# Attention and a softplus feed-forward on one core: new constants for the planner that orders the work of five engines

## The chip, the cores and the metric

One core of a Trainium2 chip runs the whole kernel. The metric is device time in microseconds (us), from one execution to the next of the same program; lower is better. TensorE (PE) does the matmuls, VectorE (DVE), ScalarE (ACT) and GpSimd (POOL) the element work, SyncE (SP) and GpSimd's queue start most transfers.

## What is computed

```python
def reference(q, k, v, moe_w_in, moe_w_out):          # float32
    # q, k, v: 8 batches, 8 heads, 576 positions, 64 wide, in 9 chunks of 64
    scores = q_c @ k_c.T / sqrt(64)                   # inside each chunk
    attn = softmax(scores)
    x = (attn @ v_c), heads side by side              # 4608 tokens x 512
    h = x @ w_in                                      # 512 x 2048
    g = maximum(h, 0) + log1p(exp(-abs(h)))           # softplus
    return g @ w_out                                  # 4608 x 512
```

## The kernel before

**Tiles and stages.** The 4608 tokens are 36 tiles of 128 (a tile is two chunks, all heads), in nine rows of four tiles (m = 0 to 8). The 2048 hidden columns are 16 pieces (fc). A block is one m with one fc, named m * 16 + fc. Each float32 product is made of three matmuls of rounded parts (hi times hi, hi times lo, lo times hi), so each operand needs a high part (a copy) and a low part (a subtraction). The first three rows run plainly, piece by piece: `gemm1` (line 640: x times w_in), softplus (line 648), its high and low part `g_hi` (line 652) and `g_lo` (line 656), then `gemm2` (line 830: g times w_out) one block later. The first two blocks are halved: half-blocks a0 and a1 use tiles 0 and 1, blocks 0 and 1 then use tiles 2 and 3. The other six rows run two at a time, in three supers, with products of sums (line 776) built from sums over x (lines 754, 761 and 766) and over w_in.

**Attention.** Tiles 0 to 3 go through TensorE one by one (transposes, scores, maximum, exp, sum, `att_norm`, transpose, product with v, high and low part of x at lines 617 and 621). The others go in pairs of tiles through bursts: `burst` multiplies the weights of one pair of tiles with v (line 604) and computes the scores of the next pair (line 516). Bursts stand at blocks 4, 8, 15 and then at `BURST_AT`, later at places inside the supers. q and k of these tiles are turned by VectorE (lines 493 and 503), the weights by VectorE too (line 540), in some tiles partly by transfers (line 551, those not in `SWAP_DVE`).

**Weight decode.** The 32 weight pieces are units, in the order in0, in1, out0, in2, out1, in3, out2 and so on: unit 3 is in2, unit 4 is out1. A unit is loaded by SP into one of three raw tiles, shifted by two bytes (`w_load`, lines 269 and 274). Then its top half (`w_top`, line 282, on ScalarE if in `TOP_ACT`, else GpSimd) and its low half (`w_low`, line 292, ScalarE) are taken out, added on VectorE (`w_add`, line 297), copied to the high part (`w_hi`, line 324, on GpSimd if in `HI_POOL`) and subtracted to the low part (`w_lo`, line 328, on GpSimd if in `LO_POOL`). All 32 are decoded while the first sixteen blocks run.

**The order.** Every step is a task of `Plan` with an engine, a cost, the tasks it needs, buffers that it takes, and an urgency `urg`. A list scheduler plays the tasks through in modelled time, and each engine's instructions are emitted in the order in which it picked them; the engines then run that order, waiting for one another by semaphores:

```python
can = [t for t in wait[eng] if ready[t["name"]] <= now + 1e-9 and has_room(t, now)]
...
t = min(can, key=lambda t: (t["urg"], t["seq"]))
...
if t["port"]:
    end = port = max(now, port) + cost
```

The last two lines are the planner's account of an exclusion between VectorE and GpSimd: every GpSimd task has `port`, and of VectorE's tasks only `w_add` has it. Plain block g is due at `30 + 5.2 * g`; a unit's urgency is its block's due time less 4 plus `DECODE_AT[u]` (for out pieces the block is later by `WO_AFTER`), a load's is that less `LEAD` or, for the first ones, taken from `LOAD_AT` (q and k of tiles 0 to 3, v of tiles 0 to 3, then units 0 to 5). Tile i of the first four has urgency `ATT_AT[i]` and up. For a burst due at d, q and k have `d - QK_URG`, v `d - V_URG`, or `d + V_LATE` if it has a place of its own (`HOMES`), swaps `d - SW_URG`; the sums over x have `d - X_URG`. In the plain rows the sums over w_in (lines 695 to 715) and the stores of w_in's parts (line 726) to a scratch tensor have `d + W_URG`. `ON_POOL` names the q, k and v that GpSimd's queue loads instead of SP. `NORM_POOL` and `GLO_POOL` name the tiles and blocks whose normalisation and whose g_lo GpSimd does, `TK` the tiles whose turned k VectorE copies instead of ScalarE. After 120 us of modelled time an engine may stay idle up to `HOLD` for an urgent task. TensorE's order of blocks and bursts is fixed in a list; it takes its PSUM from two `pa` tiles (scores, gemm1, x) and four `po` tiles (gemm2).

## Time and profile before

| | |
|---|---|
| time, median of 3 runs | 836.19 us (836.0 to 836.98) |
| profiled execution: its own time, its span | 835.88 us, 833.9 us |
| TensorE, VectorE, ScalarE, GpSimd busy | 819.0, 522.3, 382.0, 327.6 us |
| granted TensorE clock | 1.00 |
| first matmul of gemm1 | 24.46 us |
| burst at block 4, 8, 15, 22 starts | 52.47, 78.20, 122.64, 163.03 us |
| first product of the three supers | 316.30, 487.58, 660.80 us |

The span goes from the first to the last instruction of the profiled execution; the time also holds what lies around it. Busy time of TensorE counts its pipelined matmuls with modelled ends, so a busy TensorE says only that matmuls follow one another.

### The profile page before, as it was taken

To read this page: it belongs to the slowest core of one execution; us is meant where nothing else is said; L and a number is where in the kernel's file an instruction comes from. 1 tells how busy PE (TensorE), PEld (TensorE's weight loads), DVE (VectorE), ACT (ScalarE), POOL (GpSimd) and SP (SyncE) were. 2 spreads that over 40 slices of the span, in tenths; PEclk is the share of its full clock that TensorE was granted. 3 is DMA by queue.
4 is the path that set the end of the run, shared out by engine and by line. 5 is a ranking of instruction groups with operands and counts; after the bars stand their busy time and mean duration, and the time that the engine had idled before them with its cause. 6 is when DMAs were issued, how large, how long until landed. Compare 5 with 4: busy or idle time off the path is not lost.

```text
span 833.9 us, 15342 instructions
## 1 busy us (share of the span) xinstructions
PE 819.0 (98%) x5745; PEld 671.3 (80%) x5745; DVE 522.3 (63%) x871; ACT 382.0 (46%) x612; POOL 327.6 (39%) x380
## 2 busy tenths in 40 slices
PE   9899999999999999999999999999999999999998
PEld 7677778888888878888887878888888888888886
DVE  3998987178568677475577877583867732232322
ACT  4867764345443564353444544433544443333322
POOL 1654569776998652311324521232230021311100
PEclk9999999999999999999999999999999999999999
DMA  9997657755475455777558427758452155354332
GB/s 215 259 211 171 185 164 206 221 115 168 87 192 124 111 150 189 190 217 201 161 187 217 112 91 234 192 168 241 140 200 92 51 208 183 115 181 159 101 101 75
DMA packets 189513, 137.34 MB, mean 165 GB/s; under 512 B 152704, under 2 KB 166272, under 8 KB 186496
## 3 DMA queue, kind: packets, MB, share of 16 engines
q1 hardware_dynamic: 178400, 86.68, 39.0%
q0 software_dynamic: 10896, 49.56, 19.0%
q8 instruction: 45, 0.74, 0.4%
q14 instruction: 28, 0.23, 0.1%
q10 hardware_dynamic: 144, 0.13, 0.0%
HBM read 100.14 MB, written 35.13 MB: 162 GB/s over the span
## 4 chain that ended last, share of the span: by engine, by line
PE 84%; DVE 5%; DMA 4%; SPq 3%; issue 1%; ACT 1%; POOL 1%; DVEq 0%; POOLq 0%
PE po L830 42%; PE pa L776 27%; PE pa L640 11%; PE pa L604 2%; DMA q<-in_q_dram 2%; SPq L355 2%; PE pa L516 2%; DMA raw<-in_moe_w_out_dram 1%; DMA raw<-in_moe_w_in_dram 1%; DVE qe L503 1%; DVE ends L297 1%; DVE wib L297 1%; SPq L551 0%; POOL g_lo L656 0%; SPq L269 0%
## 5 line engine op out<-in xcount | busy, mean ns | idle before, releaser
L795 POOL TENSOR_TENSOR wib<-wib 128x512 f32<-128x512 f32 x48 | 63.5, 1323 | 279.1 <-ACT wib L782 273.8
L830 PE MATMUL po<-late,g_hi 128*128 128x512 f32 x538 | 165.8, 391 | 0.0
L656 DVE TENSOR_TENSOR g_lo<-ends,g_hi 128x512 fp32r<-128x512 f32 x96 | 66.3, 691 | 92.1 <-ACT g_hi L652 88.2
L830 PEld LDWEIGHTS po<-late,g_hi 128*128 128x128 f32 x538 | 100.3, 188 | 21.3 <-DVE late L328 0.3
L776 PE MATMUL pa<-wi_hi,xb 128*128 128x512 f32 x368 | 113.4, 389 | 0.0
L652 ACT CAST g_hi<-ends 128x512 fp32r<-128x512 f32 x96 | 59.3, 618 | 114.0 <-PE po L830 108.5
L830 PE MATMUL po<-wo_hi,g_hi 128*128 128x512 f32 x288 | 109.7, 393 | 0.6 <-POOL wo_hi L324 0.6
L830 PE MATMUL po<-wo_lo,g_hi 128*128 128x512 f32 x288 | 108.7, 390 | 0.6 <-POOL wo_lo L328 0.6
L830 PE MATMUL po<-late,g_lo 128*128 128x512 f32 x287 | 108.1, 390 | 1.0 <-issue 0.7
L830 PE MATMUL po<-wo_hi,g_lo 128*128 128x512 f32 x288 | 108.5, 389 | 0.0
L776 PE MATMUL pa<-wib,xb 128*128 128x512 f32 x432 | 104.2, 394 | 0.7 <-DVE wib L766 0.7
L540 DVE STREAM_TRANSPOSE eT<-qe 32x256 f32<-32x256 f32 x224 | 97.4, 435 | 5.1 <-POOL qe L591 1.9
L776 PEld LDWEIGHTS pa<-wib,xb 128*128 128x128 f32 x432 | 79.2, 188 | 21.8 <-ACT wib L782 5.5
L795 DVE TENSOR_TENSOR wib<-wib,pa 128x512 f32<-128x512 f32 x72 | 49.4, 686 | 62.0 <-PE pa L776 47.3
L776 PEld LDWEIGHTS pa<-wi_hi,xb 128*128 128x128 f32 x368 | 68.9, 188 | 14.5 <-issue 0.2
L776 PE MATMUL pa<-wi_lo,xb 128*128 128x512 f32 x184 | 71.6, 389 | 0.0
L648 ACT ACTIVATE u<-pa 128x512 f32<-128x512 f32 (+1 forms) x50 | 29.0, 580 | 87.3 <-PE pa L640 80.1
L782 ACT COPY wib<-pa 128x512 f32<-128x512 f32 x72 | 39.8, 588 | 62.4 <-PE pa L776 62.4
L803 ACT ACTIVATE ends<-pa 128x512 f32<-128x512 f32 x48 | 28.7, 598 | 80.9 <-PE pa L776 55.7
L830 PEld LDWEIGHTS po<-late,g_lo 128*128 128x128 f32 x287 | 53.9, 188 | 13.1 <-issue 1.1
L830 PEld LDWEIGHTS po<-wo_lo,g_hi 128*128 128x128 f32 x288 | 54.0, 188 | 12.1 <-POOL wo_lo L328 1.1
L830 PEld LDWEIGHTS po<-wo_hi,g_hi 128*128 128x128 f32 x288 | 53.7, 188 | 12.0 <-POOL wo_hi L324 0.8
(184 smaller groups left out, 1362.5 us busy)
## 6 DMA issues: line engine op xcount, KB each, us to landing
xb<-scratch POOLq DMA_DIRECT2D x23, 1024.0 KB, 5.6
xb<-scratch POOLq DMA_DIRECT2D x24, 768.0 KB, 7.3
spill<-ends SPq DMA_DIRECT2D x21, 512.0 KB, 5.7
ends<-spill SPq DMA_DIRECT2D x21, 512.0 KB, 3.3
out_dram<-raw SPq DMA_DIRECT2D x35, 256.0 KB, 2.8
raw<-in_moe_w_in_dram SPq DMA_DIRECT2D x16, 512.0 KB, 5.3
raw<-in_moe_w_out_dram SPq DMA_DIRECT2D x16, 512.0 KB, 4.6
scratch<-ends SPq DMA_DIRECT2D x16, 512.0 KB, 3.4
```

Of the source, the lines that this page charges most:

```text
L297: nc.vector.tensor_tensor(low, low, live.pop(("top", u)), op=ALU.add)
L355: eng.dma_start(dst[p0 : p0 + rows], src[b, :, s0 : s0 + rows, :].rearrange("h s d -> s h d"))
L540: nc.vector.transpose(live["eT", i][d : d + BL, tb], e[s : s + BL, kb])
L640: nc.tensor.matmul(ph, wt[:, c, :], x[:, ts_, c, :], start=(n == 0), stop=(n == 3 * KC - 1))
L648: nc.scalar.activation(w["u"], w["ph"], AF.Softplus)
L652: nc.scalar.copy(w["hi"], w["u"])
L656: (nc.gpsimd if pool else nc.vector).tensor_tensor(w["lo"], w["u"], w["hi"].bitcast(F32), op=ALU.subtract)
L776: nc.tensor.matmul(w["bank"][BANK[k]], wts[:, q, c, :], x[:, c, :], start=k < NX and c + n == 0, stop=c == 1 and n == 2, skip_group_check= ...
L782: nc.scalar.copy(tmp_of(n), w["bank"][n])
L795: (nc.gpsimd if what in MIX_POOL else nc.vector).tensor_tensor(out, a, b, op=op)
L803: nc.scalar.activation(u_tiles(j)[i], src, AF.Softplus)
L830: nc.tensor.matmul(pos[w["m"]][t], terms[n][0][:, j * P : (j + 1) * P], terms[n][1], start=(w["first"] and n == 0), stop=n == 2 and (w["la ...
```

## The change

Constants only. Sets that choose an engine: `TK`, `HI_POOL`, `LO_POOL`, `TOP_ACT`, `NORM_POOL`, `GLO_POOL`, `SWAP_DVE`, `ON_POOL`. Urgencies and places: `DECODE_AT`, `ATT_AT`, `LOAD_AT`, `WO_AFTER`, `QK_URG`, `V_URG`, `V_LATE`, `W_URG`, `X_URG`, `SW_URG`, `LEAD`, `HOLD`, and the third of `BURST_AT`, from block 31 to 32. No function is edited; every engine's order comes out of the planner anew.

```diff
--- before.py
+++ after.py
@@ -41,7 +41,7 @@
     FLYING = 8
     AHEAD = 3.2
     WARM_UNTIL = 90.0
-    HOLD = 0.55
+    HOLD = 0.5
     HOLD_FROM = 120.0
 
     def __init__(self, **pools):
@@ -869,17 +869,17 @@
     NOFF = 3
     T0 = 30.0
     TG = 5.2
-    DECODE_AT = (-10.4, -5, -1, -3, -5, 1, -3, 3, -40.8, -60, 2.4, -5)
-    TK = ()
+    DECODE_AT = (-20, -2.3, -8.9, -2, -60, 1.4, 0.2, -3, 2.1, -5, 5.9, 0)
+    TK = (1, 2)
     KS = 0.2
-    ATT_AT = (-34.3, -4.4, -52.4, -194.6)
-    LOAD_AT = (-89.2, -65.7, -51.7, -58.6, -27.7, -49.7, -47.4, -42.4, -48.8, -0.1, -8.7, 2.1, 5.1, 35.8)
-    HI_POOL = (0, 1, 2, 3, 4, 5, 6, 7, 11, 13, 16, 18, 19, 20, 21, 24, 25, 30, 31)
+    ATT_AT = (-52.5, 101.4, -70.6, -226.8)
+    LOAD_AT = (-104.1, -66.1, -54.8, -64.2, -28.7, -42.9, -41.8, -37.3, -47.5, -9.7, -24.4, -1.0, -1.7, 22.2)
+    HI_POOL = (0, 1, 2, 3, 5, 6, 7, 8, 11, 12, 13, 15, 17, 18, 19, 20, 21, 25, 31)
     WHOLE = (4, 5, 9)
-    SWAP_DVE = (4, 7, 8, 10, 11, 12, 13, 14, 15, 16, 17, 19, 20, 21, 22, 23, 24, 25, 26, 27, 28, 29, 30, 31, 32, 33, 34, 35)
+    SWAP_DVE = (4, 7, 9, 10, 11, 13, 14, 15, 16, 17, 19, 20, 21, 22, 23, 24, 25, 26, 27, 28, 29, 30, 31, 32, 33, 34, 35)
     SWAP_ACT = ()
     BEGIN = (4, 8, 15)
-    BURST_AT = (22, 26, 31, 36, 40, 44)
+    BURST_AT = (22, 26, 32, 36, 40, 44)
     HOMES = {(n, i): ("early", 2 * (i - FIRST_BLK) + j) for i in (5, 7) for j, n in enumerate("qk")}
     HOMES.update({("v", 4): ("early", 4), ("v", 5): ("early", 5)})
     HOMES.update({("v", 8): ("xb", 0), ("v", 9): ("xb", 1), ("q", 11): ("xb", 4), ("k", 11): ("xb", 5)})
@@ -899,12 +899,12 @@
         ("v", 10, 0, (0, 1)), ("v", 11, 0, (0, 1)), ("q", 13, 0, (2, 3)), ("k", 13, 0, (2, 3)),
         ("v", 16, 1, (0, 1)), ("v", 17, 1, (0, 1)), ("v", 18, 1, (2, 3)), ("v", 19, 1, (2, 3)))})
     LOAD_POOL = ()
-    TOP_ACT = (1, 4, 5, 6, 7, 8, 9, 11, 12, 13, 15, 17, 18, 19, 21, 22, 24, 25, 26, 28, 29, 30, 31)
+    TOP_ACT = (1, 4, 5, 6, 7, 8, 9, 12, 13, 14, 15, 17, 18, 19, 20, 22, 24, 25, 26, 28, 30)
     LOAD_AFTER = "q0"
-    LO_POOL = (2, 3, 4, 8, 9, 11, 13, 17, 19, 21, 23, 25, 26, 28)
-    NORM_POOL = (0, 3, 4, 5, 6, 8, 10, 15, 18)
-    GLO_POOL = (0, 1, 2, 7, 8, 10, 13, 14, 15, 17, 18, 19, 21, 22, 23, 26, 30, 34, 35, 36, 38, 42, 44, 45, 47)
-    WO_AFTER = 1.3
+    LO_POOL = (2, 3, 4, 7, 9, 11, 12, 13, 14, 17, 18, 19, 22, 23, 26, 29, 31)
+    NORM_POOL = (0, 3, 4, 5, 6, 8, 10, 13, 14)
+    GLO_POOL = (0, 3, 6, 7, 8, 10, 13, 17, 19, 20, 21, 22, 23, 25, 26, 34, 39, 44)
+    WO_AFTER = 1.1
     IN_SUPER = ([0, 2], [0, 5], [0, 7], [1, 4])
     XS_POOL = ()
     XL_POOL = ()
@@ -913,18 +913,18 @@
     QK_AFTER = "v3"
     V_AFTER = "load10"
     K6_AFTER = "load13"
-    QK_URG = -16.8
+    QK_URG = -54.3
     T_URG = -0.6
-    V_URG = 26.0
-    V_LATE = 27.1
-    W_URG = 7.6
+    V_URG = 111.0
+    V_LATE = 31.9
+    W_URG = 0.2
     QUEUE = dict(wd="SP", wo="SP", ring="POOL", us="SP", ul="SP")
     ISSUE = dict(ACT=0.4, SP=0.57, POOL=0.6)
-    ON_POOL = (['k', 11], ['k', 14], ['k', 15], ['k', 17], ['k', 30], ['q', 16], ['q', 21], ['q', 29], ['q', 30], ['v', 8], ['v', 10], ['v', 11], ['v', 16], ['v', 20], ['v', 21], ['v', 26], ['v', 27], ['v', 29], ['v', 33], ['v', 34], ['v', 35])
+    ON_POOL = (['k', 9], ['k', 11], ['k', 15], ['k', 17], ['k', 29], ['q', 10], ['q', 14], ['q', 16], ['q', 21], ['q', 30], ['v', 8], ['v', 11], ['v', 12], ['v', 13], ['v', 16], ['v', 24], ['v', 26], ['v', 27])
     LOADER = {(n, i): "POOL" for n, i in ON_POOL}
-    X_URG = 97.0
-    SW_URG = -34.0
-    LEAD = 5
+    X_URG = 130.5
+    SW_URG = -57.4
+    LEAD = 9.39571158947384
 
     blocks = [
         dict(m=m, fc=fc, first=fc == 0, last=fc == FC - 1, g=m * FC + fc, name=m * FC + fc, tiles=range(TPM))
```

## Rows read from the trace of the kernel before

**Rows 1.** Windows: stretch, length, busy us (count) of PE, PEld, DVE, ACT, POOL; then TensorE clock.
```profile
0.00:24.00 24.00, 21.61 (x286) 17.90 (x286) 10.82 (x23) 12.16 (x21) 5.77 (x12) 1.00 1.09 229
24.00:122.00 98.00, 91.02 (x646) 73.31 (x647) 91.19 (x153) 69.65 (x114) 52.37 (x49) 1.00 0.76 196
122.00:300.00 178.00, 178.00 (x1612) 147.40 (x1611) 115.09 (x207) 82.82 (x129) 142.71 (x166) 1.00 0.59 157
300.00:833.90 533.90, 528.41 (x3205) 432.63 (x3203) 305.24 (x491) 217.39 (x350) 126.79 (x153) 1.00 0.53 159
```

**Rows 2.** TensorE in order of time: start, us, instruction, [idle before <-releaser].
```profile
29.86 0.71 PE L640 MATMUL pa<-xb,wi_hi 128*128 128x256 f32 x4 [1.45 <-DVE xb L621]
...
34.93 0.73 PE L830 MATMUL po<-wo_hi,g_hi 128*128 128x512 f32 x2 [0.58 <-POOL wo_hi L324]
36.29 0.74 PE L830 MATMUL po<-wo_lo,g_hi 128*128 128x512 f32 x2 [0.63 <-POOL wo_lo L328]
...
40.14 1.07 PE L640 MATMUL pa<-xb,wi_hi 128*128 128x512 f32 x4
...
76.17 2.09 PE L640 MATMUL pa<-xb,wib 128*128 128x512 f32 x8 [0.69 <-DVE wib L328]
...
114.80 1.45 PE L640 MATMUL pa<-xb,wib 128*128 128x512 f32 x5 [1.06 <-DVE wib L328]
```

**Rows 3.** VectorE in order of time, decode instructions of the ramp.
```profile
28.42 0.70 DVE L328 TENSOR_TENSOR wi_lo<-wib,wi_hi 128x512 fp32r<-128x512 f32 x1
...
57.93 0.68 DVE L297 CUSTOM_DVE_ANT_0 wib<-wib,ends 128x1024 uint16<-128x1024 uint16 x1
...
59.85 0.68 DVE L328 TENSOR_TENSOR wo_lo<-wib,wo_hi 128x512 fp32r<-128x512 f32 x1
...
74.70 1.42 DVE L328 TENSOR_TENSOR wib<-ends,wib 128x512 fp32r<-128x512 f32 x1
...
112.90 1.24 DVE L297 CUSTOM_DVE_ANT_0 ends<-ends 128x1024 uint16<-128x1024 uint16 x1
```

**Rows 4.** The window 24 to 122 us, decode adds (line 297) alone.
```profile
24.00:122.00 98.00, 24.27 (x31) 1.00 0.76 196
```

**Rows 5.** The same window, decode subtracts (line 328) alone; VectorE, then GpSimd.
```profile
24.00:122.00 98.00, 15.60 (x15) 19.36 (x14) 1.00 0.76 196
```

**Rows 6.** The same window, softplus low parts (line 656); VectorE, then GpSimd.
```profile
24.00:122.00 98.00, 7.93 (x9) 10.14 (x8) 1.00 0.76 196
```

**Rows 7.** GpSimd in order of time, four of its instructions.
```profile
31.41 1.30 POOL L328 TENSOR_TENSOR wi_lo<-wib,wi_hi 128x512 fp32r<-128x512 f32 x1
...
58.67 0.78 POOL L282 CAST ends<-raw 128x512 f16<-128x512 bf16 x1 [3.02 <-DVE wib L297]
...
304.88 3.51 POOL L656 TENSOR_TENSOR g_lo<-u,g_hi 128x512 fp32r<-128x512 f32 x1 [6.67 <-ACT g_hi L652]
...
315.18 1.28 POOL L656 TENSOR_TENSOR g_lo<-u,g_hi 128x512 fp32r<-128x512 f32 x1 [0.56 <-ACT g_hi L652]
```

**Rows 8.** TensorE in order of time, beside the third row of rows 7.
```profile
308.44 0.50 PE L830 MATMUL po<-late,g_lo 128*128 128x512 f32 x1 [0.38 <-POOL g_lo L656]
```

**Rows 9.** SP in order of time: DMA issues of the start.
```profile
16.84 0.98 SPq L269 DMA_DIRECT2D raw<-in_moe_w_in_dram  x2
...
23.22 1.19 SPq L274 DMA_DIRECT2D raw<-in_moe_w_out_dram  x1
```

**Rows 10.** SP in order of time, ahead of the burst at block 22.
```profile
124.48 4.94 SPq L486 DMA_DIRECT2D q<-in_q_dram  x8
...
153.95 4.77 SPq L486 DMA_DIRECT2D xb<-in_q_dram  x8
158.77 3.21 SPq L726 DMA_DIRECT2D scratch<-wib  x4
```

**Rows 11.** VectorE in order of time, tile 11 before that burst.
```profile
161.18 0.71 DVE L493 STREAM_TRANSPOSE qe<-xb 128x512 f32<-128x512 f32 x1 [6.83 <-DMA scratch<-wib]
```

**Rows 12.** TensorE in order of time, scores of tile 11 in that burst.
```profile
164.79 0.68 PE L516 MATMUL pa<-ka,qe 64*64 64x64 f32 x31
```

## Prediction

> **What bounds the kernel now.** I read the windows first, to see where TensorE is idle [rows 1]: 24.00 - 21.61 = 2.4 us in the first 24 us, 98.00 - 91.02 = 7.0 us from 24 to 122, nothing from 122 to 300, and 533.90 - 528.41 = 5.5 us after that, much of it the last store behind the last matmul. The granted clock is 1.00 throughout. Both kernels do the same work, so the most that an order can win is about 7 us in the stretch from 24 to 122, in which the weights are decoded while the first block row already runs (the ramp, below), and a little behind it.
>
> TensorE's timeline then says what ends its waits there [rows 2]. The first block's second half-block, at 29.86, waits for VectorE's xb: that is the release of a `pa` bank. The second product of the ramp waits twice for GpSimd's decode of out1, 0.58 us before 34.93 and 0.63 before 36.29. At 76.17 and 114.80 the matmuls wait 0.69 and 1.06 us for VectorE's low part of a w_in piece. VectorE is the engine behind the ramp: it is busy 91.19 of 98 us, ScalarE 69.65, GpSimd 52.37 [rows 1].
>
> Part of what keeps VectorE busy is not its own work. Instructions of one form take two durations: a decode subtract (L328) 0.68 us at 59.85 and 1.42 at 74.70, a decode add (L297) 0.68 us at 57.93 and 1.24 at 112.90 [rows 3]. Over the ramp, against 0.68 us each: 24.27 - 31 x 0.68 = 3.2 us for the adds, 15.60 - 15 x 0.68 = 5.4 us for the subtracts, and 7.93 - 8 x 0.68 = 2.5 us for g_lo, two of whose nine are half-size [rows 4 to 6]. About 11 us of VectorE's 91 are stretch. It comes from GpSimd, and it works both ways: the g_lo that GpSimd began at 304.88, beside VectorE's sums over x, took 3.51 us, the one at 315.18 took 1.28 [rows 7]. The Trainium skill (SBUF — State Buffer, Who interferes with whom) states the rule: a VectorE instruction with two SBUF inputs and a GpSimd instruction that reads SBUF exclude each other, and the later one waits for the whole of the other. The trace agrees: 3.51 against 1.28 us.
>
> **The change part by part.** All of it is constants: sets that choose an engine, and urgencies that choose an order.
>
> *Engines in the ramp.* LO_POOL gains units 7, 12, 14, 18, 22, 29, 31 and loses 8, 21, 25, 28. Unit 31 is decoded after 122 us, so two low parts net leave VectorE: -2 x 0.68 = -1.4 us there, +2 x 1.28 = +2.6 us on GpSimd. GLO_POOL up to block 16 loses 1 (a half block), 2, 14, 15 and gains 3, 6, one and a half blocks net: +1.0 us on VectorE, -1.9 us on GpSimd. TOP_ACT drops 11, 21, 29, 31 and takes 14, 20: two tops net, 2 x 0.78 = +1.6 us on GpSimd [rows 3, 7]. HI_POOL swaps four for four. VectorE's own work changes by -0.4 us, GpSimd's by +2.3 us. GpSimd's 52 us stretched VectorE by 11, or 0.21 us for each; 2.3 x 0.21 = +0.5 us. Together +0.1 us: the moves by themselves are worth nothing.
>
> *TK.* Two copies of kT go from ScalarE to VectorE before 16 us. VectorE is busy 10.82 of the first 24 us [rows 1]; its idle time hides them. Without that cover they would cost about 0.7 us each.
>
> *Loads of units 3 and 4.* The new urgencies put unit 4 (out1) ahead of unit 3 (in2), and give unit 4's decode -60. A load needs one of three raw tiles: in2 was the second of the pair issued at 16.84, out1 came at 23.22 [rows 9]. Exchanged, out1 is some 6 us earlier and both its waits go: -0.58 - 0.63 = -1.2 us. in2 is 6 us later: its low part was done at 31.41 + 1.30 = 32.7 on GpSimd [rows 7], so 38.7, and its first matmul stood at 40.14 [rows 2], or 38.9 with TensorE 1.2 us earlier. in2 is late next, by nothing yet. Bounds -1.2 to 0; I take -1.2, as the two rows are 0.2 us apart on the good side.
>
> *Tile 1 of the attention last.* Its urgency goes from -4.4 to 101.4, behind tiles 0, 2 and 3 and the first decodes, and the first block needs tiles 0 and 1. What can be put ahead of it on VectorE is the work of two tiles, some five instructions of 0.7 us: at most +3 us. The other way, tiles 2 and 3 finish earlier and the 1.45 us before 29.86 go; but that matmul also needs unit 1, whose low part ended at 28.42 + 0.70 = 29.12 [rows 3], so at most -0.7. I take 0: unit 1 sets this point either way.
>
> *The order around the stretch.* Two VectorE instructions directly ahead of TensorE's waits were stretched: the subtract at 74.70 by 0.74 us, ahead of a wait of 0.69; the add at 112.90 by 0.56, ahead of one of 1.06 [rows 2, 3]. An order that keeps GpSimd from beside them wins the smaller of each pair, 0.69 + 0.56 = 1.25 us. Bounds: 0 (others are stretched instead) and -5.8 (all the ramp's 7.0 us but the 1.2 above). I take -1.25, the only waits whose rows show a stretch right before them.
>
> *g_lo of blocks 42, 45, 47 to VectorE.* Block 45's is the one of 3.51 us, and TensorE waited 0.38 us for it [rows 7, 8]. On VectorE its urgency (-1) puts it ahead of the sums over x, at 0.69 us: -0.4 us. The other g_lo moved to VectorE behind the ramp are hidden: it is busy 115 of 178 us from 122 to 300 [rows 1].
>
> *Transfers.* QK_URG, V_LATE, SW_URG, W_URG, ON_POOL and the swaps of tiles 8, 9 and 12 reorder SP's queue from 115 us on. TensorE is never idle from 122 to 300, so nothing can be won there; what can be lost is the third rival. LEAD brings loads from unit 6 on forward by 4.4 us of urgency, but free raw tiles hold them back: nothing. X_URG, V_URG and HOLD: what they move was first in its queue already, or is not in front of TensorE: nothing; the bound is the 5.5 us of idle time behind 300 us, tail included.
>
> Sum: 0.1 - 1.2 + 0 - 1.25 - 0.4 = -2.75 us. The profiled execution took 835.88 us (833.9 of span, 2.0 around it), so 833.1; it lies 0.3 us below the median of 836.19. Forecast: **833.4 us**. No change is taken as within 0.2%, 1.7 us: 834.5 to 837.9.
>
> **The rivals.**
>
> *The ramp's gain is swallowed.* VectorE is behind the ramp's last wait too, the one before 114.80. If it gets through its 91 us no sooner, what is won at 35 us is lost again there, and only the 0.4 us at 308 remain: 835.8. For it speaks that the moves come to +0.1 us; against it that 11 of the 91 us are stretch, which an order can change.
>
> *VectorE and GpSimd together fill the ramp (slower).* GpSimd's 52 us and VectorE's 55 adds, subtracts and g_lo at 0.68 us, 37 us, exclude each other: 89 of 98 us. Each low part moved adds 1.28 - 0.68 = 0.6 us to that, each top 0.78, each g_lo moved back takes off 0.6: 1.2 + 1.6 - 0.9 = +1.9 us. From the point at which that sum, and not VectorE alone, is what the ramp goes by, the time is 836.2 + 1.9 = 838.1. A rule of the Trainium skill (Perfetto Trace Analysis, Optimizing Scalar/DVE Operations) warns of it: offloading from VectorE to GpSimd might not help, since they share a read port.
>
> *A burst waits for its q (slower).* q of tile 11 was issued at 153.95, ahead of four weight stores at 158.77 that took 3.21 us of SP; its transpose ended at 161.18 + 0.71 = 161.9, and the burst used it at 164.79 [rows 10 to 12]. By the new urgencies (due 144.4 + 54.3 = 198.7, against 161.4 for these stores and 176.3 for v of tile 10) the stores and four transfers of v go first, 3.2 + 2.5 us, while q of tile 10 (4.9 us) leaves SP for GpSimd: 0.8 us later, in time by 2.1, with TensorE some 2.4 us earlier. If q10's move frees nothing, the burst stands 5.7 - 2.9 = 2.8 us, and the gains being there or not, 836.2 or 839.
>
> *The first block starts late (slower).* If tile 1 is done later than unit 1 (29.12), each us goes straight to the end: with +3 us and no gain but the 0.4, 838.8.
>
> **How the numbers follow.** The forecast's case 0.44, its own range 830.5 to 834.5. Swallowed 0.25 (834.6 to 837). Both engines 0.11 (837 to 839, half of it past 837.9). A burst 0.12 (836 to 840, two thirds past). The first block 0.08 (836 to 839, most of it past). Faster 0.44, slower 0.06 + 0.08 + 0.06 = 0.20, same 0.36. For 8 in 10 the range reaches into all of them: 830.0 to 838.8.
>
> **What would show it.** Right: no wait for wo_hi and wo_lo near 35 us; TensorE idle 4.5 us or less from 24 to 122; adds and subtracts nearer 0.68 us in the mean; block 45's g_lo on VectorE. Wrong: the first block later than 27 us with nothing won behind it; idle time before a burst's L604 or L516 between 160 and 300 us; VectorE as full and as stretched as before, up to 120 us.

## The result, and the profile after

The changed kernel takes 838.02 us (median of 15 executions, 836.18 to 841.15) against 836.19 for the kernel before on the same chip (15 executions, 835.18 to 837.81): a ratio of 1.0025, 95% interval 1.0013 to 1.0037. It is slower by 1.8 us, where 833.4 was forecast. The time lies inside the range, the direction is wrong.

The profiled execution took 840.45 us, its span is 838.7; it is one of the longer ones. The windows, to be set against [rows 1]:

```profile
0.00:24.00 24.00, 21.59 (x278) 17.72 (x278) 11.36 (x21) 9.71 (x17) 4.57 (x11) 1.00 1.11 233
24.00:122.00 98.00, 90.86 (x661) 75.16 (x653) 89.40 (x154) 67.71 (x112) 56.41 (x54) 0.98 0.72 193
122.00:300.00 178.00, 176.07 (x1572) 145.35 (x1574) 111.22 (x200) 80.66 (x127) 142.69 (x174) 1.00 0.58 154
300.00:839.00 539.00, 533.15 (x3264) 436.20 (x3255) 303.24 (x497) 221.47 (x354) 105.62 (x126) 1.00 0.53 159
```

VectorE is relieved a little in the ramp (91.19 to 89.40 us) and GpSimd is busier by 4.0, yet TensorE is no busier. Two things are new: the granted clock is 0.98 there, and from 122 to 300 us, where TensorE had no idle time, it now has 1.93 us. A busy share doesn't place the loss, so the next reading sets the start of the same matmul in both traces against each other:

| place (start before, us) | after - before, us |
|---|---|
| first half-block, G1_a0 (24.46) | +2.07 |
| second half-block, G1_a1 (29.86) | +5.43 |
| first gemm2 (31.37) | +6.47 |
| block 2 (40.14) | +4.71 |
| block 14 (112.67) | +1.33 |
| block 15 (119.50) | +2.20 |
| 168.25 | +2.22 |
| 256.70 | +4.15 |
| 310.86 | +3.46 |
| end of the third super (805.49) | +4.72 |

So the ramp behind its start does gain, 4.71 - 1.33 = 3.4 us; all of that and more was lost ahead of it, and 1.93 us are lost once more near 250 us. What is left of the 4.72 is small: +0.87 at block 15, -0.69 near 308 us and +1.26 in the supers, where the largest wait, 0.88 us before 413.22, has no releaser in the trace. TensorE's timeline shows both main losses, and answers [rows 2]:

```profile
26.53 0.72 PE L640 MATMUL pa<-xb,wi_hi 128*128 128x256 f32 x4
...
33.86 1.78 PE L375 MATMUL pa<-ident 128*128 128x128 f32 x8 [1.96 <-DVE xb L621]
35.29 1.20 PE L640 MATMUL pa<-xb,wi_hi 128*128 128x256 f32 x4
...
37.84 0.62 PE L830 MATMUL po<-wo_hi,g_hi 128*128 128x512 f32 x2
...
117.03 2.12 PE L640 MATMUL pa<-xb,wib 128*128 128x512 f32 x8 [1.84 <-DVE wib L328]
...
255.32 0.47 PE L640 MATMUL pa<-xb,wi_hi 128*128 128x512 f32 x1 [1.77 <-DVE qe L566]
```

The two waits for wo_hi and wo_lo near 35 us are gone, as forecast, and so is the one of 0.69 us before 76.17. Two waits of the kernel before that the prediction did not list, at the bursts of blocks 4 and 8, are gone with it:

```profile
57.55 1.16 PE L640 MATMUL pa<-xb,wi_hi 128*128 128x512 f32 x4 [0.55 <-DVE qe L566]
...
80.83 0.69 PE L516 MATMUL pa<-ka,qe 64*64 64x64 f32 x32 [0.66 <-DVE ka L493]
```

These three places are most of the 3.4 us (0.71, 0.86 and 0.87 us of it). The wait before 114.80, of 1.06 us, has grown to 1.84 in this execution (117.03). And the wait for VectorE's xb, 1.45 us before 29.86, is now 1.96 before 33.86. It is the same bank of `pa`: it holds tile 3's x until VectorE's xl3 (line 621) has read it. ScalarE and VectorE in order of time say why that is late:

```profile
27.29 0.78 ACT L282 CAST ends<-raw 128x512 f16<-128x512 bf16 x1
27.94 0.66 ACT L292 ACTIVATE wib<-raw 128x512 int32<-128x512 uint32 x1
28.61 1.28 ACT L648 ACT_TABLE_LOAD   x1
29.91 0.38 ACT L648 ACTIVATE u<-pa 128x256 f32<-128x256 f32 x1
30.19 0.58 ACT L617 CAST xb<-pa 128x512 fp32r<-128x512 f32 x1
```

```profile
29.53 1.14 DVE L297 CUSTOM_DVE_ANT_0 wib<-wib,ends 128x1024 uint16<-128x1024 uint16 x1
30.59 0.68 DVE L328 TENSOR_TENSOR wi_lo<-wib,wi_hi 128x512 fp32r<-128x512 f32 x1
31.29 1.79 DVE L503 STREAM_TRANSPOSE qe<-q 32x256 f32<-32x256 f32 x4
33.11 1.29 DVE L621 TENSOR_TENSOR xb<-pa,xb 128x512 fp32r<-128x512 f32 x2
```

Unit 4, decoded early now, puts its top and low half (27.29 and 27.94) ahead of the softplus and its table load on ScalarE, so tile 3's xh3 runs at 30.19. VectorE meanwhile takes unit 4's add, unit 1's low part (28.42 before, [rows 3]) and the q transpose Tq4, 1.79 us long, and xl3 follows at 33.11. TensorE has nothing to do, and the eight filler matmuls (line 375) that the planner put ahead of G1_a1 write the same bank, so they wait for it too and then take 35.29 - 33.86 = 1.43 us more. That makes up the 3.36 us by which G1_a1 is later than G1_a0: 0.39 is G1_a0 itself, whose last matmuls wait until 27.82 for tile 1's low part, 1.54 lies between tile 3's product with v (28.53, before 26.07) and the end of the wait (33.86, before 29.86), 1.43 is the filler. The granted clock in steps of 2 us from 32:

```profile
32.00:34.00 2.00, 0.14 (x1) 0.14 (x2) 1.94 (x5) 2.00 (x5) 0.68 (x1) 1.00 0.22 82
34.00:36.00 2.00, 2.00 (x11) 2.00 (x12) 1.99 (x5) 0.61 (x2) 0.60 (x1) 0.55 0.61 173
36.00:38.00 2.00, 2.00 (x12) 2.00 (x11) 0.99 (x3) 0.00 (x0) 1.28 (x2) 0.59 0.89 313
```

TensorE was busy 0.14 of 2 us, and the clock then fell to about half, the 1.2 GHz level. G1_a1 took 37.84 - 35.29 = 2.55 us; before, 31.37 - 29.86 = 1.51. The filler was slowed too, as the experiment with q21 will show. The sum to block 2: 2.07 + 3.36 (G1_a1 behind G1_a0) + 1.04 (clock, in G1_a1 alone) - 1.76 (out1's waits) = 4.71.

The loss at 255 us begins on VectorE with one g_lo; GpSimd's rows stand beside it:

```profile
249.95 3.90 DVE L656 TENSOR_TENSOR g_lo<-u,g_hi 128x512 fp32r<-128x512 f32 x1 [3.53 <-ACT g_hi L652]
```

```profile
246.12 4.61 POOL L486 DMA_DIRECT2D xa<-in_q_dram  x8 [3.82 <-DVE qe L493]
250.75 2.55 POOL L695 TENSOR_TENSOR raw<-wib 128x512 f32<-128x512 f32 x2
253.37 3.13 POOL L707 TENSOR_TENSOR ends<-raw 128x256 f32<-128x256 f32 x4
```

The g_lo, 0.69 us when nothing disturbs it, starts 0.80 us ahead of two two-input instructions of GpSimd that follow its issues of q21, and ends 0.55 us behind the second, though GpSimd's next additions, at 253.37, begin before that. The burst's maxima queue behind it on VectorE, and TensorE waits 1.77 us. The transfer itself is in time; issuing it from GpSimd at that place, as the kernel before did at another moment, is what did harm.

### The profile page after: what moved, and what is told of

It is laid out like the page before. It is cut to its first block, busy times and chain, and to the rows that moved or that the text cites. A ratio compares the mean times of both kernels' runs of the same rounds, so it can differ in the third digit from the quotient of the medians.

```text
span 838.7 us, 15358 instructions
## 1 busy us (share of the span) xinstructions
PE 821.7 (98%) x5751; PEld 674.4 (80%) x5751; DVE 515.2 (61%) x870; ACT 379.5 (45%) x608; POOL 309.3 (37%) x363
## 4 chain that ended last, share of the span: by engine, by line
PE 86%; DVE 7%; ACT 2%; DMA 2%; issue 1%; POOL 0%; SPq 0%; DVEq 0%; POOLq 0%; ACTq 0%
PE po L830 42%; PE pa L776 26%; PE pa L640 13%; PE pa L604 2%; PE pa L516 1%; DVE ends L297 1%; DMA xb<-scratch 1%; DVE qe L503 1%; PE po L375 1%; DVE g_lo L656 1%; DMA spill<-ends 1%; PE po L416 1%; DVE eT L540 0%; ACT u L648 0%; DVE wib L795 0%
## 5 line engine op out<-in xcount | busy, mean ns | idle before, releaser
L540 DVE STREAM_TRANSPOSE eT<-qe 32x256 f32<-32x256 f32 x216 | 93.9, 435 | 3.0
L830 PEld LDWEIGHTS po<-wo_hi,g_lo 128*128 128x128 f32 x288 | 54.1, 188 | 11.4
```

Source lines behind the costliest of these rows:

```text
L540: nc.vector.transpose(live["eT", i][d : d + BL, tb], e[s : s + BL, kb])
L830: nc.tensor.matmul(pos[w["m"]][t], terms[n][0][:, j * P : (j + 1) * P], terms[n][1], start=(w["first"] and n == 0), stop=n == 2 and (w["la ...
```

## The experiments

Each kernel was timed against the kernel before on the same chip:

| kernel | us, median (range, executions) | before | ratio, 95% interval |
|---|---|---|---|
| changed kernel | 838.02 (836.18 to 841.15, 15) | 836.19 | 1.0025, 1.0013 to 1.0037 |
| tile 2 behind | 835.51 (834.48 to 837.20, 11) | 835.81 | 0.9999, 0.9991 to 1.0008 |
| no filler | 836.19 (832.71 to 839.73, 12) | 835.81 | 1.0011, 0.9998 to 1.0024 |
| q21 on SP | 836.25 (833.31 to 839.74, 12) | 835.81 | 1.0006, 0.9990 to 1.0021 |
| q14 and q21 on SP | 835.61 (833.11 to 838.78, 12) | 835.94 | 0.9995, 0.9983 to 1.0006 |
| old engines | 838.81 (837.95 to 844.13, 6) | 835.49 | 1.0054, 1.0032 to 1.0075 |
| tile 2 behind, q14, q21 on SP | 835.69 (834.03 to 838.22, 12) | 835.49 | 1.0001, 0.9991 to 1.0011 |
| tile 2 behind, tile 3 first | 835.81 (833.70 to 838.46, 12) | 836.41 | 0.9997, 0.9985 to 1.0009 |
| all three | 832.77 (832.32 to 834.54, 6) | 835.49 | 0.9970, 0.9958 to 0.9982 |

A constant set back alone makes the planner order everything anew, so that nothing is held still. The edits below change the emitted order in a few places and leave the rest; taking q14 and q21 off GpSimd left the planner's modelled end as it was. That modelled end, no measurement, is itself 0.4 us later with the new constants than with the old.

Starts against the kernel before, in each kernel's own profile, in us:

| place | changed | again | tile 2 behind | no filler | old engines | q14, q21 on SP | all three |
|---|---|---|---|---|---|---|---|
| G1_a0 | +2.07 | +2.33 | +1.57 | +0.42 | +0.96 | +0.96 | +1.16 |
| G1_a1 | +5.43 | +5.44 | +2.93 | +2.00 | +3.36 | +4.60 | +0.71 |
| block 2 | +4.71 | +4.96 | +3.10 | +1.77 | +1.62 | +3.72 | +0.90 |
| block 14 | +1.33 | +1.54 | +0.66 | -1.67 | +0.32 | +0.25 | -1.37 |
| 168.25 | +2.22 | +0.74 | -0.64 | -3.10 | +0.60 | -0.89 | -1.71 |
| 203.15 | +2.22 | +2.82 | -0.64 | -1.14 | +0.60 | -0.88 | -1.71 |
| 256.70 | +4.15 | +4.79 | -0.73 | +0.81 | +2.55 | -0.97 | -1.79 |
| 805.49 | +4.72 | +5.40 | -1.12 | +1.74 | +2.87 | -0.30 | -1.69 |

**The changed kernel again**, unedited: a second profile, 841.14 us.

> The changed kernel once more, unedited, for a second profile. If the late start is a property of the order, half-block a1 starts again some 5 us later than in the kernel before (35.3 against 29.9 us), and the stall of 1.9 us in front of the block after the burst at 40 is there again. If these are accidents of one execution (the runs of the changed kernel spread over 5 us, those of the kernel before over 2.6), a1 is within 2 us of 29.9 or the stall is missing.

The start is the same (+5.44 at G1_a1), and so is the loss at 250 us. The wait before block 15 is absent; a new one of 1.78 us stands at 203, behind another g_lo held by GpSimd's chain, VectorE's row first, then GpSimd's:

```profile
198.60 4.91 DVE L656 TENSOR_TENSOR g_lo<-u,g_hi 128x512 fp32r<-128x512 f32 x1 [2.11 <-issue]
```

```profile
195.98 3.45 POOL L486 DMA_DIRECT2D q<-in_q_dram  x6
199.44 1.30 POOL L695 TENSOR_TENSOR raw<-wi_hi,wi_lo 128x512 f32<-128x512 f32 x1
200.69 1.05 POOL L591 TENSOR_TENSOR qe<-qe,den 128x512 f32<-128x512 f32 x1
201.69 1.26 POOL L695 TENSOR_TENSOR raw<-wi_hi,wi_lo 128x512 f32<-128x512 f32 x1
```

Here the issues are those of q14. What is common to both executions is the start and the kind of stall; which stalls fall due differs.

**Tile 2 behind.** Tile 2's product and x parts are emitted behind G1_a1, which has no need of them:

```diff
+moved = [p for p in out if p[1]["name"] in ("V2", "xh2", "xl2")]
+out = [p for p in out if p[1]["name"] not in ("V2", "xh2", "xl2")]
+n = [p[1]["name"] for p in out].index("G1_a1") + 1
+out[n:n] = moved
```

> The changed kernel with the v product of attention tile 2 and its two x parts emitted right behind half-block a1 instead of ahead of it, so that a1 no longer waits for the release of that PSUM tile. Theory A (the late start passes through to the end): a1 starts near 31.3 us, when unit 1 is decoded, 4 us earlier than 35.3; the first blocks and the time follow by 2 us or more (836 or less). Theory B (VectorE's decode sets TensorE's place at 122 us): a1 is as early, but the block at 119.5 + 2.2 us stands within 0.7 us of there, and the time changes by less than 0.8 us.

G1_a1's shift is now 1.36 us larger than G1_a0's, not 3.36; TensorE is kept going by filler from 30 us, and the clock stays up. The window of the profile:

```profile
30.00:32.00 2.00, 2.00 (x19) 2.00 (x20) 1.94 (x4) 1.69 (x4) 1.47 (x2) 1.00 1.19 309
```

G1_a1 comes at 32.79 and not near 31.3, as expected: unit 1's low part is done at 30.84 and the bank is free, but 26 filler matmuls, emitted for the longer planned gap, run from 29.86 on. They keep the clock up and delay the matmul that they stand ahead of. Not all of the gain is kept either: block 0's other half, which needs tile 2, now waits in its turn (+4.66 where G1_a1 has +2.93), so that at block 2 the shift is 1.5 us larger than at G1_a0, against 2.6. The time falls to that of the kernel before, 2.5 us below the changed kernel's, as theory A has it; theory B's block at 119.5 would stand near +2.2 and is at -0.74. In its profile the g_lo of the 250 us stall, which VectorE starts 0.81 us ahead of GpSimd's chain this time, escapes; VectorE, then GpSimd:

```profile
247.09 0.69 DVE L660 TENSOR_TENSOR g_lo<-u,g_hi 128x512 fp32r<-128x512 f32 x1 [3.52 <-ACT g_hi L656]
```

```profile
243.27 4.61 POOL L490 DMA_DIRECT2D xa<-in_q_dram  x8 [3.82 <-DVE qe L497]
247.90 2.55 POOL L699 TENSOR_TENSOR raw<-wib 128x512 f32<-128x512 f32 x2
```

**No filler** ahead of G1_a1 (other filler stays):

```diff
-self.gap = start - last if start < self.WARM_UNTIL else 0.0
+self.gap = start - last if start < self.WARM_UNTIL and t["name"] != "G1_a1" else 0.0
```

> The changed kernel without the eight filler matmuls in front of half-block a1. They wait for the same PSUM tile as a1 does, so they run behind the wait and not in it. If they matter only by their own time, a1 starts 1.4 us earlier (33.9) and everything up to the next wait with it. If the low clock behind the idle stretch (0.55 of full from 34 to 36 us) is what costs, it falls on a1's own matmuls instead, and the gain at the next block is under 0.8 us. Theory A: what is won there shows in the time; theory B: it does not (under 0.5 us).

G1_a1's shift is 1.58 us larger than G1_a0's, 1.8 less than in the changed kernel, and it starts at the 1.2 GHz level all the same. TensorE's row, and the window of it:

```profile
31.86 1.20 PE L640 MATMUL pa<-xb,wi_hi 128*128 128x256 f32 x4 [1.60 <-DVE xb L621]
```

```profile
32.00:34.00 2.00, 2.00 (x10) 2.00 (x11) 1.99 (x5) 1.32 (x2) 0.61 (x1) 0.50 0.64 198
```

Here the filler, which waits for the same bank, did not keep the clock up (0.55 with it, 0.50 without); it only delayed the matmul behind it. The time, 1.0011, can't be told from no change, nor surely from the changed kernel's; this profile has both stalls, at 198 and 250 us.

**q21 on SP:**

```diff
-    ON_POOL = (..., ['q', 16], ['q', 21], ['q', 30], ...)
+    ON_POOL = (..., ['q', 16], ['q', 30], ...)
```

> The changed kernel with q of tile 21 loaded through SP instead of GpSimd's queue; nothing ahead of 200 us is touched by it. If the g_lo of block 40 took 3.9 us because GpSimd was issuing that load and went on to two sums over w_in, those run earlier, g_lo takes 0.7 to 2 us, and the wait of 1.8 us in front of the next block goes: 1 to 2 us off the time if the wait is in every execution. If the wait has another cause, or is an accident, it stays, or the time stays within 0.5 us.

There is no stall near 250 us in its profile (833.38 us); the g_lo takes 0.83 us. The ratio is 0.0019 below the changed kernel's, less than either interval is wide. The start of this profile shows what the clock costs. Its order and its filler there are those of the changed kernel, but VectorE's add of unit 4 took 0.69 us and not 1.14, the wait is shorter by that, and the clock stayed up:

```profile
32.02 1.16 PE L375 MATMUL pa<-ident 128*128 128x128 f32 x8 [1.51 <-DVE xb L621]
```

```profile
32.00:34.00 2.00, 1.98 (x17) 1.99 (x18) 1.99 (x5) 1.24 (x3) 0.44 (x1) 1.00 0.45 136
```

The filler took 32.93 - 32.02 = 0.91 us and G1_a1 1.52, against 1.43 and 2.55: the low clock costs 1.55 us in all. Block 2 is only 0.67 us later against G1_a0 than before, where the two profiles of the changed kernel have 2.64 and 2.63. TensorE does wait 1.26 us at 305.73 for block 45's g_lo, which stands behind VectorE's sums over x in this order.

**Old engines.** The new order, instruction for instruction, with `w_top`, `w_hi` and `w_lo` on the engines that they had before:

```diff
-nc.gpsimd.tensor_copy(hi, t) if u in HI_POOL else nc.scalar.copy(hi, t)
+nc.gpsimd.tensor_copy(hi, t) if u in EMIT_HI_POOL else nc.scalar.copy(hi, t)
...
+EMIT_HI_POOL, EMIT_LO_POOL, EMIT_TOP_ACT = # the sets HI_POOL, LO_POOL, TOP_ACT of the kernel before
```

> The changed order is kept instruction for instruction, but the decode steps w_top, w_hi and w_lo of every unit run on the engine that they had before (the lists HI_POOL, LO_POOL and TOP_ACT of the kernel before); the g_lo, normalise and DMA choices stay the new ones. Theory A (the new order itself removes the waits of the ramp; which engine decodes is a detail): from block 2 to block 14 the kernel still gains 2.4 to 3.5 us on the kernel before, as the five profiles so far do, and the time is within 1 us of the changed kernel's, about 1.001 to 1.003 of the time before. Theory C (the gain of the ramp comes from the moved decode steps, and VectorE and GpSimd are the bound that they relieve): the gain from block 2 to block 14 falls to less than 1 us, and the kernel ends some 2.5 to 3.5 us behind the changed one, at 839 to 842 us (1.005 to 1.007). A third way, that order and engines only work together, would show as new waits of TensorE for decoded tiles between 40 and 115 us, each of 0.5 us or more.

The waits for out1 stay away (+3.36 at G1_a1, +1.62 at block 2); but from block 2 to block 14 only 1.62 - 0.32 = 1.3 us are gained, not 3.4, and the ratio is 1.0054. TensorE's waits in its profile:

```profile
85.46 0.93 PE L640 MATMUL pa<-xb,wib 128*128 128x512 f32 x3 [1.79 <-DVE qe L566]
...
253.71 0.47 PE L640 MATMUL pa<-xb,wi_hi 128*128 128x512 f32 x1 [1.77 <-DVE qe L566]
```

Ahead of the first, VectorE does a low part (82.95, 1.04 us) that the changed kernel gives to GpSimd, before the burst's maximum; there the same wait is 0.60 us. So some 2.1 of the 3.4 us need the moved decode steps, and theory A's "a detail" falls; theory C's "less than 1 us" does not come either, but its ratio does. As this order was planned for the new engines, the experiment shows what order and engines do together, not what the moves would do in the old order. The stall at 250 us is the same as in the changed kernel.

**Tile 2 behind, and q14 and q21 on SP:** the edit of tile 2, and

```diff
-    ON_POOL = (..., ['q', 10], ['q', 14], ['q', 16], ['q', 21], ['q', 30], ...)
+    ON_POOL = (..., ['q', 10], ['q', 16], ['q', 30], ...)
```

> The changed kernel with tile 2's V2, xh2 and xl2 behind G1_a1 as in the earlier experiment, and in addition the loads of q14 and q21 issued from SP instead of GpSimd. Theory A with the hand-over (a late start that passes through, and stalls where VectorE's g_lo meets GpSimd's chain behind a DMA issue): G1_a1 starts 1 to 3 us behind the kernel before, and no stall of TensorE of over 1 us at 195 to 205 or 246 to 256 us; the median falls by up to 1 us below the 835.5 of tile 2 alone, to 834.3 to 835.5, and the spread of the timed runs is narrower than the 5 to 6 us of the changed kernel. Theory D (the stalls are chance and move elsewhere): the same median as with tile 2 alone, 835.5 plus or minus 0.5, and a stall of 1.5 us or more at another place in the stretch of 120 to 310 us.

The profile has no stall over 1 us at 200 or 250 us, as expected, but the median is that of tile 2 alone, and the spread, 4.2 us, is narrower than the changed kernel's 5.0 and wider than tile 2 alone's 2.7. The lower median was missed; theory D has the median right, but the stall that it wants elsewhere between 120 and 310 us is not in the profile, whose largest wait there is 0.69 us.

**All three**: besides, VectorE's xl3 goes ahead of Tq4, and the filler ahead of G1_a1 is cut to the gap that is left:

```diff
+out[n:n] = xl3                    # n: place of Tq4
...
+if t["name"] == "G1_a1":
+    self.gap = 2.2
```

> As the kernel with tile 2 behind and q14 and q21 on SP, and VectorE's xl3 is put ahead of its q transpose Tq4, with the filler ahead of G1_a1 cut to the shorter gap. Theory A (each us of the start goes straight to the end): G1_a1 starts about 1.3 us earlier than with tile 2 alone, against G1_a0 of the same run some 5 us behind it, and the end comes 0.5 to 1.4 us earlier: 833 to 834.5 us, 0.997 to 0.999 of the time before. Theory B (VectorE sets the place of TensorE by 107 us, whatever the start): G1_a1 earlier, and blocks 9 to 14 and the end where they are without it, within 0.4 us. If Tq4, now 0.7 us later, is what a burst waits for next, blocks 2 to 5 show a wait for qe of up to 0.7 us and the gain is halved.

The first matmul of G1_a1, and the window of the ramp:

```profile
30.57 0.71 PE L649 MATMUL pa<-xb,wi_hi 128*128 128x256 f32 x4
```

```profile
24.00:122.00 98.00, 93.39 (x732) 76.25 (x732) 90.77 (x154) 70.00 (x117) 59.92 (x56) 1.00 0.74 197
```

Against the kernel without the third edit, G1_a1 is 2.0 us earlier (+0.71 against +2.71); so are block 2 (+0.90 against +2.90) and block 14 (-1.37 against +0.58), and the end is 1.6 earlier. By the rows the 2.0 us are the filler's, 10 matmuls from 29.43 to 30.57 where 26 stood; what xl3 ahead of Tq4 adds was not run apart. The profiled execution, 834.04, is one of the longer of its six. At 832.77 us this kernel beats both: 0.9970 of the kernel before. The shift passes the ramp one to one; theory B, that VectorE takes back by 107 us what the start gains, falls.

**Tile 2 behind and tile 3 first** without the edit of `ON_POOL`: q14 and q21 come from GpSimd, as in the changed kernel.

> The kernel with tile 3 first and tile 2 behind, but q14 and q21 issued from GpSimd as the changed kernel has them. Theory A with the start as the whole gain: 832.3 to 833.5 us, within 0.5 us of the kernel with tile 3 first (832.77), no stall over 1 us of TensorE at 195 to 205 or 246 to 256 us in most executions, since tile 2 alone showed none either. Theory A with the hand-over: some of the executions, those whose g_lo falls on the hand-over, take 1.9 or 3.8 us more, so that the median is 833.5 to 836 and the spread 4 us or more.

The second theory's figures hold: 835.81 us, 0.9997, and a spread of 4.8. The start is the same as with all three (+0.66 at G1_a1, -1.63 at block 14). At 250 us the stall is back, and the shift goes from -3.05 to -1.10. VectorE's row:

```profile
244.68 3.90 DVE L665 TENSOR_TENSOR g_lo<-u,g_hi 128x512 fp32r<-128x512 f32 x1 [3.52 <-ACT g_hi L661]
```

**q14 and q21 on SP alone**, the edit of `ON_POOL` and no other.

> The changed kernel with q14 and q21 issued from SP and nothing else. Theory A with the stalls as a separate cost: G1_a1 starts as late as in the changed kernel, 2 to 5 us behind the kernel before, no stall over 1 us at 195 to 205 or 246 to 256 us, and the median falls by 1 to 3 us against the changed kernel, to 0.9985 to 1.001 of the time before (834.9 to 837.0). Theory with the start as the whole cost: 1.0015 to 1.0035, 837.4 to 839.1.

G1_a1 is late as ever (+4.60, and the clock is at 0.50 from 34 to 36 us), no g_lo is held, and the median is 0.9995: two edits, each without the other, bring the changed kernel back to the time before, though only one of them touches the start.

**The stall by itself.** A kernel that computes nothing of the reference: rounds of one VectorE reduction of growing length and one subtraction, beside four DMA issues (or four copies) and three additions on GpSimd.

```python
nc.vector.tensor_reduce(red, wide[:, :cols], axis=AX.X, op=ALU.max)
nc.vector.tensor_tensor(lo, a, b, op=ALU.subtract)
...
for n in range(3):
    nc.gpsimd.tensor_tensor(sums[n], a, b, op=ALU.add)
```

> A measurement of the disputed stall by itself; this kernel computes nothing of the reference, it writes a constant tile to the output. Each round releases VectorE and GpSimd by one ScalarE copy. VectorE then runs a reduction of 600 to 3475 columns, in steps of 125, and one subtraction of two 128x512 tiles; GpSimd issues four DMAs of 32x512 and then three additions of two 128x512 tiles, or, in the other half of the rounds, four plain copies in place of the DMA issues. The subtraction alone took 0.69 us in the kernel, the addition 1.27. Theory E (a two-input instruction of VectorE that stands between GpSimd's DMA issue and GpSimd's chain of two-input instructions is held until the chain ends): in the rounds with DMAs one or two neighbouring steps show a subtraction of 3.9 to 4.9 us, in those with copies none shows over about 2 us. Rival F (the two engines take turns instruction by instruction, whatever stands ahead): no subtraction over about 2 us in either half. Rival G (any subtraction that meets the start of a chain is held for all of it): one or two long ones in both halves.

Two rounds with DMA issues and one with copies, VectorE's subtraction and GpSimd's additions:

```profile
116.81 0.68 DVE L188 TENSOR_TENSOR lo<-a,b 128x512 f32<-128x512 f32 x1
...
130.16 5.00 DVE L188 TENSOR_TENSOR lo<-a,b 128x512 f32<-128x512 f32 x1
...
137.56 1.80 DVE L188 TENSOR_TENSOR lo<-a,b 128x512 f32<-128x512 f32 x1
```

```profile
130.90 3.69 POOL L201 TENSOR_TENSOR sum<-a,b 128x512 f32<-128x512 f32 x3
...
137.55 4.15 POOL L201 TENSOR_TENSOR sum<-a,b 128x512 f32<-128x512 f32 x3
```

In 16 of the 24 rounds with DMA issues the subtraction took 3.04 to 5.00 us; it ended some 0.56 us behind the last of the three additions, wherever among them it had begun. In the other 8 it began 0.86 us or more ahead of the first addition and took 0.68. In all 24 rounds with copies it took 0.68 to 1.80, and an addition gave way instead (the three took 4.15 us together, not 3.69). Theory E is right in kind, F and G fall; but it isn't one or two steps, the hold caught every subtraction that began from some 0.7 us ahead of the chain to 1.22 us into it, the latest here.

**The stall with other chains**, the same way: one issue or four, three additions or six, a copy or a waiting addition between.

> The measurement of the stall by itself once more; nothing of the reference is computed, a constant tile is written to the output. VectorE's one subtraction starts 1.2 or 0.6 or 0.3 us ahead of GpSimd's chain of additions, or 0.3, 0.9 or 1.5 us into it. What GpSimd does differs: four DMA issues and three additions; one issue and three; four and six; four, a plain copy and three; four, an addition that waits 0.3 to 0.5 us for ScalarE, and three; four, an addition, a copy, an addition. If a DMA issue leaves GpSimd holding what VectorE needs until GpSimd next waits (theory E2), a subtraction that starts 0.6 us ahead of the chain or later ends about 0.56 us after the last addition in all forms without a wait, up to 8.6 us with six additions, and in the form with a wait it is done within 2 us. If the hold covers a fixed time or a fixed number of additions (rival H), six additions hold it no longer than three, 4 to 5 us. If a copy between gives the turn to VectorE (rival I), the forms with a copy show no subtraction over 2.7 us.

VectorE, six additions and then the copy between; then GpSimd:

```profile
118.03 8.30 DVE L207 TENSOR_TENSOR lo<-a,b 128x512 f32<-128x512 f32 x1
...
129.67 0.96 DVE L207 TENSOR_TENSOR lo<-a,b 128x512 f32<-128x512 f32 x1
```

```profile
118.43 7.34 POOL L195 TENSOR_TENSOR sum<-a,b 128x512 f32<-128x512 f32 x6
...
129.46 0.62 POOL L198 COPY sum<-far 128x512 f32<-128x512 f32 x1
130.16 4.03 POOL L195 TENSOR_TENSOR sum<-a,b 128x512 f32<-128x512 f32 x3
```

Six additions hold it 8.30 us, and three behind a single issue 4.67, as three behind four do (4.66). So rival H falls. In the form with the waiting addition the longest is 1.78, and with a copy right behind the issues 1.73; a copy in the middle of the chain releases nothing (4.30). Theory E2 seems to hold, but its wait did not take place: in each of these rounds ScalarE was done before GpSimd came to the addition. What the two short forms share in the trace is a gap of some 0.08 us behind GpSimd's first instruction (129.46 + 0.62 = 130.08, next 130.16), which no other form has. Every long hold ended some 0.56 us behind the last instruction ahead of GpSimd's first gap, in the kernels as well: at 253.30 a gap of 0.07 us stands ahead of the additions that did not prolong the hold. A copy without such a gap releases nothing in the changed kernel either. Its g_lo at 108.14 was held through a copy (108.31 to 109.10) and a subtraction that ended at 110.31, behind one DMA issue:

```profile
108.14 2.73 DVE L656 TENSOR_TENSOR g_lo<-u,g_hi 128x512 fp32r<-128x512 f32 x1
```

So rival I falls, and the hold lasts as long as GpSimd's unbroken run. What makes the gap was not varied. Three further rounds are not explained: there VectorE began 0.08 to 0.69 us ahead of the chain and went first (0.68 to 1.02 us).

## Why the prediction was wrong, step by step

*Tile 1 of the attention last* is the step that failed. It says: "I take 0: unit 1 sets this point either way". The bound written beside it, +3 us, was passed too: G1_a1 is 5.43 us late, 3.36 us of it on top of 2.07 at G1_a0. Unit 1 did not set this point. Its low part moved itself, from 28.42 to 30.59, and TensorE's wait is for tile 3's x. The normalisation that TensorE needs ahead of G1_a0, at 22.46 before, ran at 24.52. Over the profiles with the new order G1_a0 is 0.42 to 2.33 us late, so one execution doesn't size this part: counted from GpSimd's normalisation of tile 0, whose place differs between executions too, it is 1.40 us later in both profiles of the changed kernel and 0.88 in the eight others. That it is tile 1's urgency that does this is argued from the order and not shown, as no run sets it back alone; in the planner's model, setting it back makes G1_a1 1.4 us earlier and block 14 3.7 us later. The rest comes from the step beside it, *Loads of units 3 and 4*, which counted what out1's early load takes away (1.2 us forecast; 1.76 measured) and not that its decode now stands ahead of tile 3's x: 1.32 us on ScalarE (27.29 to 28.61, with the table load behind it) and an add of 1.14 on VectorE, and that the planned order, in which xh3 is late, puts Tq4's 1.79 ahead of xl3. The rival *The first block starts late (slower)*, given 0.08, has its condition wrong and its consequence right. Tile 1's x was done at 27.82, ahead of the 29.12 that it names; the tile that came late was tile 3. But each us does go straight to the end. That is shown by the nine profiles with the new engines: they stand 0.8 to 5.0 us late at block 2 and gain 2.3 to 3.5 from there to block 14 whatever the lateness (2.3 to 2.5 in the four with tile 2 behind, 3.4 to 3.5 in the others); and by the kernel with all three edits.

The clock was in no step, nor the filler. Behind TensorE's idle 1.96 us the clock costs 1.55 us, 0.52 in the filler and 1.03 in G1_a1, by the rows of q21 on SP, where the wait was 1.51 us and the clock did not fall. It fell in both profiles of the changed kernel, and 11 of its 15 timed executions show a mean clock of 0.997 to 0.999 (838.9 us in the mean), the other four 1.000 (837.2). That fits, but other differences between executions are in it.

*The order around the stretch* was sized too small and *Engines in the ramp* at nothing. Together they brought 3.4 us from block 2 to block 14. Of the 1.25 forecast only the 0.69 before 76.17 lies there, and it came; the 0.56 before 114.80 lies behind block 14 and did not come in this execution, where the wait grew (in the second it is gone). The other two waits that went, at the bursts of blocks 4 and 8, stood in no step. With the old engines in the new order 1.3 us are left. The stretch did go down where it was looked for. The window from 24 to 122 us for lines 297, 328 and 656, which answers [rows 4 to 6]:

```profile
24.00:122.00 98.00, 24.69 (x30) 0.98 0.72 193
...
24.00:122.00 98.00, 10.81 (x13) 21.42 (x16) 0.98 0.72 193
...
24.00:122.00 98.00, 8.02 (x9) 8.92 (x7) 0.98 0.72 193
```

The subtracts on VectorE take 0.83 us in the mean instead of 1.04; the adds, 0.82 against 0.78, do not gain. *VectorE and GpSimd together fill the ramp* did not come: GpSimd rose by 4.0 us, more than the 2.3 forecast, and the ramp is faster behind its start. *The ramp's gain is swallowed* came in part, by the longer wait before block 15, in the profiled execution and not in the second.

*g_lo of blocks 42, 45, 47*: right. Block 45's takes 0.69 us on VectorE, and the place gains 4.15 - 3.46 = 0.69 (0.4 forecast), though in the order of q21 on SP it is late again. *TK* was not free: TensorE waits 0.51 us before 16.71 for VectorE's copy (line 404), where the kernel before has no wait. What that adds to G1_a0's lateness isn't separated.

*Transfers* had the second hole: "TensorE is never idle from 122 to 300, so nothing can be won there; what can be lost is the third rival". No burst waits for its q (in five of the profiles the one at block 15 waits for its v, 0.24 to 0.51 us). What was lost is 1.66 to 1.78 us of waiting a time, once or twice in a profile, because a q is issued from GpSimd just ahead of a chain of its two-input instructions, where a g_lo of VectorE now stands: q14's issue is new there, q21's was there before, and only its neighbours in time have changed. In [rows 7] stood a long hold the other way round, a GpSimd g_lo of 3.51 us, and no price was drawn from it for VectorE. The prediction read it as a wait for one instruction; in the trace it waited through two whole sums of VectorE, those at 304.88 and 306.02, to 307.24, until VectorE paused for 0.44 us. With q14 and q21 back on SP the changed kernel falls from 1.0025 to 0.9995.

The two losses don't add up cleanly. Tile 2 behind or q14 and q21 on SP, either alone, gives the 1.8 us back; both together give no more than one; with tile 3 first as well, 2.7 us are gained on the kernel before. Whether a g_lo is caught turns on less than a tenth of a us, and not on that alone: one that began 0.84 us ahead of the chain was caught (198.60, second profile), one at 0.81 escaped, others at 0.81 were caught. So an edit of the start may also decide which stalls fall due; that this explains the kernel with both edits isn't shown, since the one execution of it in a profile has no such stall. Open too is the spread of 4 to 7 us that most of these kernels have, where the kernel before has 2.6 in 15 executions; the clock's fall and the stalls, which come and go between executions, are each of the size to make part of it.

## What to carry to other kernels

An instruction stream moved earlier is paid for by what stands behind it on every engine it crosses: where a list is reordered, list the instructions now ahead of the first thing that TensorE waits for, table loads and transposes among them, before its waits are booked as gains. Filler needs a bank that is free, or it waits with the matmul that it is to keep warm, and no more of it than the gap that is really there, or it delays that matmul. And a DMA issue on GpSimd is not only its own 0.58 us: look at what GpSimd does next, and which VectorE instruction stands there.

## What was not expected of the hardware

Behind DMA issues on GpSimd, a chain of its two-input instructions is not shared instruction by instruction. A VectorE subtraction of two 128x512 tiles that met such a chain took 2.7 to 4.9 us in the kernels and up to 8.30 alone; behind copies without issues, at most 1.80. It is not so each time: at five places of the kernels such a chain gave way to a g_lo that began 0.12 to 0.64 us inside it (1.18 to 1.35 us). Every long hold ended some 0.56 us behind the last instruction ahead of GpSimd's first gap of 0.07 us or more; what makes such a gap, and who is caught, is not settled. The Trainium skill (SBUF — State Buffer, Who interferes with whom) has the loser of the shared pair wait for the whole of one instruction. The rounds with copies agree, at 1.80 us with additions of 1.26; those with DMA issues do not, and there the measurement decides. The same section infers that such a subtraction does not itself contend with descriptor generation. Most of those that ran beside the issues agree, at 0.65 to 0.69 us; the g_lo at 225.88 of the changed kernel, 1.20 us beside issues alone, does not.
